# Six V tiles move from ahead of the first score to between the scores

## The chip, the cores and the metric

The kernel runs on one core of a Trainium2 chip. The metric is the device time of one execution in microseconds (us), the median of the runs shown. The core has five engines that work side by side, each with a queue of its own that it works off in order: TensorE (PE) does matmuls, VectorE (DVE) and ScalarE (ACT) work on tiles and read the matmuls' results from PSUM, GpSimd (POOL) works on tiles in SBUF, and SyncE (SP) issues nearly all DMAs of this kernel. Engines and DMAs wait for each other by semaphores, which are counters.

## What is computed

The input is x, 2048 tokens of 512 numbers, all in float32. The result mixes an attention block and a gated feed-forward block (FFN), token by token:

```python
g = sigmoid((x * gate_w).sum(-1, keepdims=True))
q, k, v = x @ wqkv, split into 32 heads of 16
a = softmax(q @ k.T * 16 ** -0.5) @ v, heads joined, @ wo
b = (silu(x @ w1) * (x @ w3)) @ w2        # 512 -> 1792 -> 512
out = g * a + (1 - g) * b
```

## The kernel before

**Precision.** A float32 matmul costs more than one in the reduced type float32r. The kernel therefore splits every operand of a large product into a high part (H) and the rest (L) in float32r, and adds three matmuls, H·H, H·L and L·H (`three`, line 93). Rows go through DRAM where another layout is wanted.

**First phase.** x comes in four blocks of 512 tokens (`load_x`). TensorE transposes a block (`transpose_x`), ScalarE and VectorE write its two parts (xH, xL). `project_qk(c, b, w)` computes q and k for 128 columns (chunk c, 8 heads) and block b, ScalarE rounds the high part, VectorE subtracts, and SP stores the four tiles to DRAM (`store_qk`). In the first phase this is done for chunk 0 only, in four calls, one for each block. `project_v(t)` computes V for 128 tokens and all heads in 12 dense matmuls; there are 16 such tiles, and ScalarE copies each into V. For the last three tiles (`last_v`, three PSUM banks) VectorE makes the copies behind the branch below.

**The guard.** The softmax subtracts no row maximum. Instead `bound()` takes an upper bound for all scores from the largest squared norm of a token (`x_squares`) and the weights' column norms (`squares`), and sets a flag. `guard_rows()` writes the bound as two rows per head to a DRAM tensor M. `load_guard` loads them beside the rows of q, where Kt holds -1, so that the score matmul subtracts the bound. `load_q` and `load_k` fetch the H and L rows of two heads from DRAM into the tiles Qt and Kt. Only if the flag is not set, `row_maxima()` (line 275, its branch on line 278) computes true maxima; this branch stands at the end of the first phase and is not taken with these inputs. Its body contains projections, DMAs and a `load_step(0)`, so the engines' semaphores have to agree behind it whether it was taken or skipped. All engines read the flag and branch for themselves.

**The stream.** What follows is a long order of slots, written out by hand as a string. A score is one unit: 128 keys against 512 queries of two heads (line 745), then one exponential on ScalarE (line 749). There are 1024 units, 32 in a step; a step is two heads against half of the queries. The letters are Q (one unit's scores), P (V times the exponentials of two units, line 733, which accumulates in `acc`), and F (`feed`). An F advances two lanes by one matmul each: lane 0 uses the upper 64 rows of the TensorE array, lane 1 the lower 64. A block of n slots is done by one lane for one half of the contraction and then, at least 6 ticks later (GAP), by the other lane for the other half. `blocks()` yields them in order: q and k for chunks 1 to 3, the FFN's w1 and w3 products (chunk by chunk, 12 slots a block), the FFN's second product (the h phase, 14 slots a block), and the first o products. `load_weights` loads the chunks' weights and POOL splits them; chunk 0 of this list is loaded in the first phase, ahead of the branch. `halves_of` and `load_piece` load h and split it on POOL.

One turn of the order is a period of 8 Q and 4 P. A period of kind "one" has 21 F, and one of kind "two" has 15:

```python
LONG, SHORT = 78, 50
one = "QQFFFFFF" + "QFFF" * 5 + "QPPPP"
two = "QFFF" * 5 + "QPPQQPP"
order = one * LONG + "QQFFF" + two * (SHORT - 1) + "QFFF" * 4 + "QPPQPP"
```

Two PSUM tiles hold scores (S), so a third unit's scores need the first one's exponential to be done. Three banks (f) serve the blocks and the V tiles.

**The order around the change.** Behind `project_qk(0, 3)`, SP's queue holds these items, in this order: the stores of block 3, `load_q` and `load_k` for the first step, the two stores of M, the two weight loads of chunk 0, the two guard loads, the branch. TensorE's queue holds V tiles 9 and 10, the matmuls of `bound`, V tile 11, the one of `guard_rows`, and V tiles 12 to 15.

Of the kernel before, what the change touches and what calls it, by code (L numbers as in the profile page):

```python
# [8 lines left out]
F32 = mybir.dt.float32  # L9
# [8 lines left out]
P = 128  # L18
S = 2048
D = 512  # L20
F = 1792
H = 32
DH = 16
NB = S // 512
NT = S // P
ND = D // P
NF = F // P
NPAIR = H // 2
SCALE = DH ** -0.5
SAFE = 64.0  # L30


@with_exitstack
def gated_mix_kernel(ctx: ExitStack, tc: tile.TileContext, x, wqkv, wo, w1, w3, w2, gate_w, out):
# [18 lines left out]
    nc = tc.nc  # L53
# [66 lines left out]
    def load_w(c):  # L120
        w = slot("fr", F32, (P, ND, P))
        nc.sync.dma_start(w, wqkv[:, c:c + P].rearrange("(k p) n -> p k n", p=P))
        return w
# [37 lines left out]
    def x_squares(b):  # L161
        for t in range(4):
            nc.scalar.activation(slot("sg", F32), xn[b][:, t, :], AF.Square, accum_out=x2[:, 4 * b + t:4 * b + t + 1])

    def x_gate(b):
        for t in range(4):
            nc.vector.scalar_tensor_tensor(slot("hx", F32), xn[b][:, t, :], 1.0, gw, op0=OP.mult, op1=OP.mult,
                                           accum_out=z[:, 4 * b + t:4 * b + t + 1])
# [5 lines left out]
    def project_qk(c, b, w, between=None):  # L174
        ps = psum2()
        for i in range(2):
            if i and between:
                between()
            for n, (h, xs) in enumerate(((0, xH), (0, xL), (1, xH))):
                for k in range(ND):  # L180
                    nc.tensor.matmul(ps[:, i, :], w[i][h][:, k, :], xs[b][:, k, :], start=n == k == 0,
                                     stop=n == 2 and k == ND - 1)
        hi = p1.tile([P, 2, 512], F32R, name="hi", bufs=2)
        lo = p1.tile([P, 2, 512], F32R, name="lo", bufs=2)
        nc.scalar.activation(hi, ps, AF.Copy)
        nc.vector.tensor_sub(lo, ps, hi)
        for i in range(2):
            store_qk(i, c, b, hi[:, i, :], lo[:, i, :])
# [20 lines left out]
    def project_v(t):  # L209
        nc.scalar.activation(*sums_v(t), AF.Copy)  # L210
# [35 lines left out]
            nc.sync.dma_start(M_d[:, a, :].rearrange("h (j t) -> h j t", t=512),  # L246
                              r[a][:].bitcast(F32)[:, None, :].to_broadcast([H, 4, 512]))

    def load_k(j, i):
        for h in range(2):  # L250
            r = 64 * h
            s = slice(DH * (2 * j + h), DH * (2 * j + h) + DH)
            for o, ks in enumerate((0, 0, 1)):
                nc.sync.dma_start(Kt[i][r + DH * o:r + DH * o + DH, :].bitcast(F32), QD[1][ks][s, :])

    def load_q(j, half, i):
        for h in range(2):
# [6 lines left out]
    def load_guard(j, half, i):  # L264
        for h in range(2):
            nc.sync.dma_start(Qt[i][64 * h + 48:64 * h + 50, :].bitcast(F32),
                              M_d[2 * j + h, :, 1024 * half:1024 * half + 1024])
# [81 lines left out]
    x_gate(1)  # L349
    load_x(3)  # L350
    ws = [load_w(P * c) for c in range(1, ND)]
    for t in range(4):
        project_v(t)
    transpose_x(2)
    fill_k()
    project_v(4)
    for c in range(1, ND):
        squares(ws[c - 1], c)
    x_squares(2)
    project_qk(0, 2, wq)  # L360
    x_gate(2)
    ws = [load_w(D + P * c) for c in range(1, ND)]
    for t in range(5, 8):
        project_v(t)
    transpose_x(3)
    project_v(8)
    for c in range(1, ND):
        squares(ws[c - 1], ND + c)
    x_squares(3)
    project_qk(0, 3, wq)  # L370
    load_q(0, 0, 0)
    load_k(0, 0)
    project_v(9)
    project_v(10)
    bound()
    project_v(11)
    guard_rows()
    x_gate(3)
    load_weights(chunks[0])

# [1 line left out]
    nc.vector.tensor_scalar(g, g, 1.0, None, op0=OP.add)  # L382
    nc.vector.reciprocal(g, g)
    nc.vector.tensor_scalar(omg, g, -1.0, 1.0, op0=OP.mult, op1=OP.add)
    load_guard(0, 0, 0)
    for t in range(12, NT - 3):
        project_v(t)

    last_v = [sums_v(t) for t in range(NT - 3, NT)]
    row_maxima()  # L390
    for to, src in last_v:
        nc.vector.tensor_copy(to, src)  # L392
# [12 lines left out]
    def w_product(chunk, which, b):  # L405
        def product(ps, r, n, second):
            w = chunk["w"][which]
            k, i = divmod(n, 3)
            return nc.tensor.matmul(ps, w[i == 2][r, k, :], (xL if i == 1 else xH)[b][r, k, :],  # L409
                                    start=n == 0 and not second, stop=n == 3 * ND - 1 and second)  # L410
        return product

    qk_left = 8 * (ND - 1)

# [226 lines left out]
                    yield  # L641

    def blocks():
        last = len(chunks) - 1
        turns = [(m, b) for m in range(last - 1) for b in range(NB)]
        turns += [(last - i, b) for two in ((0, 1), (2,), (3,)) for i in (1, 0) for b in two]
        for m, b in turns:
            for which in range(2):
                if m < ND - 1:
                    yield w_product(chunks[m], which, b), qk_done(m + 1, which, b), 3 * ND  # L650
                else:
                    yield w_product(chunks[m], which, b), (up_done if which else gate_done)(m - ND + 1, b), 3 * ND
                if (b, which) == (1, 0) and m < last - 1 or (m, b, which) == (last - 1, 0, 1):
                    load_weights(chunks[m + 1])
        for t in range(NT):
            for part in range(3):
                yield h_product(t, part), h_done(t, part), PART
        for t in range(NT // 2 - 2):
            yield o_product(t), o_done(t), 3 * ND

    NBLOCK = 8 * len(chunks) + 3 * NT + NT // 2 - 2
    source = blocks()

    REST, GAP = 9, 6
# [89 lines left out]


    NP = 8
    LONG, SHORT = 78, 50
    one = "QQFFFFFF" + "QFFF" * 5 + "QPPPP"
    two = "QFFF" * 5 + "QPPQQPP"
    order = one * LONG + "QQFFF" + two * (SHORT - 1) + "QFFF" * 4 + "QPPQPP"  # L760
# [4 lines left out]
    for i, c in enumerate(order):  # L765
        clock += 1 if c != "P" else 4
        if c == "Q":
            step = issued // 32 + 1
            if issued % 32 == 6 and step < 2 * NPAIR:
                assert 8 * (ND - 1) - qk_left >= 8 * min(step // 4, ND - 1)  # L770
                load_step(step)
            pend.append(score(*next(units)))
            issued += 1
            while soon and order[i + 1] == "P":
                soon.pop(0)()
            if issued % 128 == (40 if issued // 128 == 5 else 12) and 1 <= issued // 128 < 8:
                stages.append(divide((issued // 128 - 1) % 4, (issued // 128 - 1) // 4))
            if small or later and hurry:
                for _ in range(3 if hurry else 1 + (len(small) > (6 if len(over) < 8 * len(chunks) - 16 else 0))):
                    if small or later and hurry:  # L780
                        (small or later).pop(0)()
            if loads and (hurry or issued % 2 or len(over) > 8 * len(chunks) - 12):
                loads.pop(0)()
            for stage in stages[:1]:
                if next(stage, stages) is stages:
                    stages.pop(0)
        elif c == "F":
            feed()
        else:
            pv(pend[:2])  # L790
            pend = pend[2:]
# [78 lines left out]
```

## Time and profile before

| | |
|---|---|
| median of 3 runs | 1413.47 us (1412.27 to 1413.79) |
| the profiled execution | 1409.74 us |
| its span, first to last instruction | 1408.0 us |
| TensorE busy | 1399.5 us, 99% of the span |
| ScalarE busy | 1033.5 us, 73% |
| VectorE, GpSimd busy | 483.3 us (34%), 318.7 us (23%) |

All rows of the profile come from the one profiled execution. A row of the timeline gives the start in us from the span's start, the time from the first start to the last end, the engine, the line of the kernel, the operation, what it writes and reads, and how many instructions were merged; in brackets stands how long the engine sat idle before it and who ended that. "SPq" and "POOLq" mark instructions of the queue itself, such as the issue of a DMA, which are not counted as busy time. A row of a line's instructions gives shortest, middle and longest duration in ns, and the first and last start in us. A row of the windows gives, for a stretch of time, the busy time of PE, of its weight loads (PEld), of DVE, ACT and POOL, then the share of the full TensorE clock that was granted, the share of the DMA engines and GB/s.

### The profile page before, as it was taken

The numbers are of one execution on the slowest core, as the hardware profiler recorded it, in microseconds if no ns is written. First come the engines' busy times: TensorE is split into PE (matmuls) and PEld (weight loads), VectorE is DVE, ScalarE is ACT, GpSimd is POOL, SyncE is SP. The second block draws the span as 40 slices with busy tenths as digits, with TensorE's granted clock in tenths as the row PEclk, the third lists the DMA queues.
The fourth block names the chain that finished last, engine by engine and source line by source line (L and its number), as shares of the span: only waits on it lengthen the run. The fifth ranks groups of instructions, "written<-read, shape, count | busy, mean of one in ns | idle before, by whom it ended". The sixth has DMA issues, their size and how long they took to land.

```text
span 1408.0 us, 28877 instructions
## 1 busy us (share of the span) xinstructions
PE 1399.5 (99%) x11399; PEld 826.9 (59%) x11399; DVE 483.3 (34%) x1067; ACT 1033.5 (73%) x1153; POOL 318.7 (23%) x356
## 2 busy tenths in 40 slices
PE   9999999999999999999999999999999999999998
PEld 7866556656556556556566566555555555555556
DVE  5421111565555545545464554411110110110113
ACT  4547767777777777777777777788788778877880
POOL 5024443011011101110110115441223332232240
PEclk9999999999999999999999999999999999999999
DMA  7553564243123433233332246443534433354445
GB/s 195 147 129 108 125 148 122 56 126 75 38 66 86 113 55 76 58 74 91 77 76 62 82 82 156 111 106 79 124 88 91 109 105 71 69 129 109 104 120 178
DMA packets 112671, 141.44 MB, mean 100 GB/s; under 512 B 16400, under 2 KB 70672, under 8 KB 109456
## 3 DMA queue, kind: packets, MB, share of 16 engines
q1 hardware_dynamic: 110384, 135.72, 39.8%
q10 hardware_dynamic: 2144, 3.80, 0.8%
q8 instruction: 92, 1.51, 0.5%
q14 instruction: 51, 0.42, 0.1%
HBM read 90.70 MB, written 48.76 MB: 99 GB/s over the span
## 4 chain that ended last, share of the span: by engine, by line
PE 93%; DVE 0%; POOL 0%; DMA 0%; issue 0%; ACT 0%; DVEq 0%; POOLq 0%; ACTq 0%
PE acc L733 33%; PE f L409 27%; PE S L745 20%; PE f L524 11%; PE f L610 1%; PE f L95 0%; PE f L96 0%; PE f L97 0%; PE S L97 0%; PE S L96 0%; PE S L95 0%; DMA kL_d<-gs 0%; DVE V L392 0%; POOL gs L422 0%; ACT p L749 0%
## 5 line engine op out<-in xcount | busy, mean ns | idle before, releaser
L749 ACT ACTIVATE p<-S 128x1024 f32<-128x1024 f32 x1024 | 967.9, 1025 | 300.7 <-PE S L745 300.7
L733 PE MATMUL acc<-p,V 128*17 128x512 f32 x4096 | 474.4, 594 | 0.0
L745 PE MATMUL S<-Qt,Kt 50*128 50x512 f32 x2048 | 408.3, 411 | 1.0 <-DVE V L392 0.7
L745 PEld LDWEIGHTS S<-Qt,Kt 50*128 50x128 f32 x2048 | 183.9, 184 | 183.2 <-ACT p L749 85.0
L733 PEld LDWEIGHTS acc<-p,V 128*17 128x17 f32 x4096 | 102.2, 97 | 273.9 <-issue 273.6
L440 DVE RECIPROCAL sg<-sg 128x64 f32<-128x64 f32 x448 | 209.3, 517 | 49.2 <-issue 47.1
L409 PE MATMUL f<-xH,fh 64*128 64x512 f32 x1024 | 205.0, 390 | 0.5 <-DVE tick L706 0.5
L409 PE MATMUL f<-xL,fh 64*128 64x512 f32 x1024 | 205.1, 391 | 0.0
L409 PE MATMUL f<-xH,fl 64*128 64x512 f32 x1024 | 204.7, 390 | 0.0
L321 POOL CAST fh<-fr 128x512 fp32r<-128x512 f32 x32 | 19.9, 621 | 427.9 <-DMA fr<-in_B_w_dram 335.0
L409 PEld LDWEIGHTS f<-xH,fh 64*128 64x128 f32 x1024 | 99.1, 186 | 22.6 <-DVE tick L706 0.9
L409 PEld LDWEIGHTS f<-xL,fh 64*128 64x128 f32 x1024 | 99.5, 187 | 20.9
L409 PEld LDWEIGHTS f<-xH,fl 64*128 64x128 f32 x1024 | 98.3, 184 | 20.1
L706 DVE MEMSET tick<- 1x1 f32 x190 | 11.2, 59 | 273.5 <-PE f L524 156.1
L524 PE MATMUL f<-xH,fl 64*128 64x512 f32 x224 | 65.8, 390 | 0.0
L524 PE MATMUL f<-xL,fh 64*128 64x512 f32 x224 | 64.6, 390 | 0.0
L524 PE MATMUL f<-xH,fh 64*128 64x512 f32 x224 | 64.0, 391 | 0.0
L432 DVE COPY gs<-f 128x512 f32<-128x512 f32 x56 | 38.7, 691 | 69.6 <-PE f L409 63.3
L524 PE MATMUL f<-xH,raw 64*128 64x512 f32 x192 | 56.6, 390 | 0.0
L438 DVE TENSOR_SCALAR sg<-sg 128x512 f32<-128x512 f32 x56 | 27.7, 495 | 83.2 <-ACT sg L437 81.1
L714 DVE COPY u<-acc 128x512 f32<-128x512 f32 x32 | 22.1, 692 | 95.2 <-PE acc L733 88.9
L543 DVE SCALAR_TENSOR_TENSOR y<-f,omg,y 128x512 f32<-128x512 f32 x32 | 24.0, 751 | 82.9 <-PE f L524 82.9
(217 smaller groups left out, 1335.2 us busy)
## 6 DMA issues: line engine op xcount, KB each, us to landing
Kt<-kH_d SPq DMA_DIRECT2D x128, 128.0 KB
h_d<-sg SPq DMA_DIRECT2D x56, 256.0 KB
sg<-h_d SPq DMA_DIRECT2D x43, 256.0 KB
fr<-in_B_w_dram SPq DMA_DIRECT2D x42, 256.0 KB
Qt<-qH_d SPq DMA_DIRECT2D x128, 64.0 KB
Kt<-kL_d SPq DMA_DIRECT2D x64, 128.0 KB
fr<-in_A_wqkv_dram SPq DMA_DIRECT2D x18, 256.0 KB
Qt<-qL_d SPq DMA_DIRECT2D x64, 64.0 KB
```

The source lines that it names most:

```text
L321: nc.gpsimd.tensor_copy(wh, r)
L409: return nc.tensor.matmul(ps, w[i == 2][r, k, :], (xL if i == 1 else xH)[b][r, k, :], start=n == 0 and not second, stop=n == 3 * ND - 1 an ...
L432: nc.vector.tensor_copy(gs, ps)
L438: small.append(lambda: nc.vector.tensor_scalar(sg, sg, 1.0, None, op0=OP.add))
L440: small.append(lambda q=q: nc.vector.reciprocal(sg[:, q:q + 64], sg[:, q:q + 64]))
L524: ins = nc.tensor.matmul(ps, hs[t][q][i == 2][r, P * o:P * o + P], (w2L if i == 1 else w2H)[q][r, o, :], start=n == 0 and not second, stop ...
L543: nc.vector.scalar_tensor_tensor(y, ps, omg[:, t:t + 1], y, op0=OP.mult, op1=OP.add)
L610: return nc.tensor.matmul(ps, ot[t][i == 2][r, P * k:P * k + P], wo_[k][i == 1][r, :], start=n == 0 and not second, stop=n == 3 * ND - 1 a ...
L714: nc.vector.tensor_copy(u, acc)
L733: nc.tensor.matmul(acc[r:r + DH + 1, :], V[:, k, 2 * j + h, :], p[:, h, :], start=k == 0, stop=k == NT - 1)
L745: nc.tensor.matmul(ps[:, h, :], Kt[i][r:r + 50, P * k:P * k + P], Qt[i][r:r + 50, t:t + 512], start=True, stop=True)
L749: nc.scalar.activation(p, ps, AF.Exp, scale=SCALE)
```

## The change

The first phase computes V tiles 0 to 9 instead of 0 to 15. Tiles 10 to 15 become the first six blocks of the stream, 12 slots each, with their copies on VectorE. The order has 12 more periods of kind "one" and 12 fewer of kind "two", so that there are 72 more F. Conditions that counted blocks up to the end of the FFN's first products use `FIRST`, which includes the six.

The first phase is put in another order. `project_qk(0, 2)` comes ahead of the squares of the query weights, and only tiles 0 to 6 stand ahead of `project_qk(0, 3)`. `bound()` is called between the two halves (q and k) of that last projection. `load_q` and the first three blocks' columns of K are issued ahead of it, and the fourth block's columns behind it, so K takes 12 DMAs instead of 6. The guard loads come right behind M's stores, and the second piece of K and the weight loads of chunk 0 behind those. Tiles 7, 8 and 9 are now the ones whose copies stand behind the branch.

```diff
+EARLY_V = 10
-    def load_k(j, i):
+    def load_k(j, i, b0=0, b1=NB):
+        c = slice(512 * b0, 512 * b1)
...
-                nc.sync.dma_start(Kt[i][r + DH * o:r + DH * o + DH, :].bitcast(F32), QD[1][ks][s, :])
+                nc.sync.dma_start(Kt[i][r + DH * o:r + DH * o + DH, c].bitcast(F32), QD[1][ks][s, c])
...
-    for t in range(4):
+    for t in range(3):
         project_v(t)
     transpose_x(2)
     fill_k()
-    project_v(4)
+    project_v(3)
+    x_squares(2)
+    project_qk(0, 2, wq)
     for c in range(1, ND):
         squares(ws[c - 1], c)
-    x_squares(2)
-    project_qk(0, 2, wq)
+    ws = [load_w(D + P * c) for c in range(1, ND)]
     x_gate(2)
-    ws = [load_w(D + P * c) for c in range(1, ND)]
-    for t in range(5, 8):
-        project_v(t)
+    project_v(4)
+    x_squares(3)
+    project_v(5)
     transpose_x(3)
-    project_v(8)
+    project_v(6)
     for c in range(1, ND):
         squares(ws[c - 1], ND + c)
-    x_squares(3)
-    project_qk(0, 3, wq)
     load_q(0, 0, 0)
-    load_k(0, 0)
-    project_v(9)
-    project_v(10)
-    bound()
-    project_v(11)
+    load_k(0, 0, 0, 3)
+    project_qk(0, 3, wq, bound)
     guard_rows()
+    load_guard(0, 0, 0)
+    load_k(0, 0, 3, NB)
     x_gate(3)
     load_weights(chunks[0])
...
-    load_guard(0, 0, 0)
-    for t in range(12, NT - 3):
-        project_v(t)
-
-    last_v = [sums_v(t) for t in range(NT - 3, NT)]
+
+    last_v = [sums_v(t) for t in range(7, EARLY_V)]
     row_maxima()
...
+    def v_product(t):
+        b, o = divmod(P * t, 512)
+
+        def product(ps, r, n, second):
+            k, i = divmod(n, 3)
+            return nc.tensor.matmul(ps, (xL if i == 2 else xH)[b][r, k, o:o + P], wv[k][i == 1][r, :],
+                                    start=n == 0 and not second, stop=n == 3 * ND - 1 and second)
+        return product
+
+    def v_done(t):
+        return lambda ps: nc.vector.tensor_copy(V[:, t, :, 0:DH], ps.rearrange("p (h d) -> p h d", d=DH))
...
     def blocks():
+        for t in range(EARLY_V, NT):
+            yield v_product(t), v_done(t), 3 * ND
...
-    NBLOCK = 8 * len(chunks) + 3 * NT + NT // 2 - 2
+    FIRST = NT - EARLY_V + 8 * len(chunks)
+    NBLOCK = FIRST + 3 * NT + NT // 2 - 2
...
-    LONG, SHORT = 78, 50
+    LONG, SHORT = 90, 38
```

More of the change, by code (lines that the diff above doesn't have):

```diff
@@ L778, in gated_mix_kernel @@
             if small or later and hurry:
-                for _ in range(3 if hurry else 1 + (len(small) > (6 if len(over) < 8 * len(chunks) - 16 else 0))):
+                for _ in range(3 if hurry else 1 + (len(small) > (6 if len(over) < FIRST - 16 else 0))):
                     if small or later and hurry:
                         (small or later).pop(0)()
-            if loads and (hurry or issued % 2 or len(over) > 8 * len(chunks) - 12):
+            if loads and (hurry or issued % 2 or len(over) > FIRST - 12):
                 loads.pop(0)()
```

## The prediction

> **What bounds the kernel now.** I read the page first (busy time, then the chain that ended last), then the order of time on TensorE to get the price of one period, and last each queue around the first score, because the change moves work from ahead of the first score to behind it.
>
> ```profile
> PE 1399.5 (99%) x11399; PEld 826.9 (59%) x11399; DVE 483.3 (34%) x1067; ACT 1033.5 (73%) x1153; POOL 318.7 (23%) x356
> PE 93%; DVE 0%; POOL 0%; DMA 0%; issue 0%; ACT 0%; DVEq 0%; POOLq 0%; ACTq 0%
> ```
>
> TensorE (PE) is busy 99% and is 93% of the chain that ended last. So each matmul slot counts, wherever it stands, and a piece of work is only cheaper if it costs fewer TensorE microseconds in its new place. The price of a period is read from the bursts of PV matmuls (line 733), one a period in the first kind ("one"), two in the second ("two"); a period of both kinds does 8 scores and 4 P.
>
> ```profile
> 879.43 3.63 PE L733 MATMUL acc<-p,V 128*17 128x512 f32 x32
> 889.92 3.63 PE L733 MATMUL acc<-p,V 128*17 128x512 f32 x32
> ...
> 1005.06 1.91 PE L733 MATMUL acc<-p,V 128*17 128x512 f32 x16
> 1014.48 1.91 PE L733 MATMUL acc<-p,V 128*17 128x512 f32 x16
> ```
>
> "One" with 21 F takes 889.92 - 879.43 = 10.49 us; "two" with 15 F takes 1014.48 - 1005.06 = 9.42 us. Six more F cost 1.07 us.
>
> **The stream: what is added.** The count of F slots goes from 78 x 21 + 3 + 49 x 15 + 12 = 2388 to 90 x 21 + 3 + 37 x 15 + 12 = 2460: 72 more, which is 6 V tiles x 12 slots. Twelve periods turn from "two" into "one", at 12 x 1.07 = **+12.84 us**. The slots left over (12) and the tail behind the periods are the same.
>
> **The front: what is removed.** The copies that follow each V tile of the first phase (line 210) give the dense price of a tile.
>
> ```profile
> 29.35 0.60 ACT L210 ACTIVATE V<-f 128x512 f32<-128x512 f32 x1 [2.20 <-PE f L97]
> 32.15 0.60 ACT L210 ACTIVATE V<-f 128x512 f32<-128x512 f32 x1 [2.20 <-PE f L97]
> ```
>
> 2.80 us a tile, so six tiles are 16.80 us of TensorE ahead of the first score. If the first score could start that much earlier, the change would gain 16.80 - 12.84 = 3.96 us. Whether it can is the question; TensorE's own rows around the first score are these.
>
> ```profile
> 63.45 0.40 PE L95 MATMUL f<-fh,xH 128*128 128x512 f32 x1
> 68.82 0.40 PE L97 MATMUL f<-fh,xL 128*128 128x512 f32 x1
> 69.37 0.48 PE L95 MATMUL f<-fh,xH 128*128 128x512 f32 x1
> 83.61 0.40 PE L97 MATMUL f<-fh,xL 128*128 128x512 f32 x1
> 84.74 0.93 PE L745 MATMUL S<-Qt,Kt 50*128 50x512 f32 x4 [0.73 <-DVE V L392]
> 86.71 0.59 PE L745 MATMUL S<-Qt,Kt 50*128 50x512 f32 x2
> 91.78 3.63 PE L733 MATMUL acc<-p,V 128*17 128x512 f32 x32
> ```
>
> The last dense V tile ends at 84.0 and the first score starts at 84.74, the first PV burst at 91.78. `project_qk(0, 3)` ended at 63.45, and behind it stood 7 V tiles (19.6 us). In the new order only three stand there (8.4 us), and what those seven covered comes into the open. That cover was for SP's queue and the branch of `row_maxima` (line 278).
>
> ```profile
> 66.81 0.45 SPq L172 DMA_DIRECT2D kL_d<-lo  x1
> 74.83 0.84 SPq L246 DMA_DIRECT2D m_d<-sg  x2
> 75.72 2.19 SPq L314 DMA_DIRECT2D fr<-in_A_wqkv_dram  x2
> 79.39 0.61 SPq L266 DMA_DIRECT2D Qt<-m_d  x2
> 84.58 0.32 SPq L261 DMA_DIRECT2D Qt<-qH_d  x1
> ...
> 88.44 0.94 SPq L254 DMA_DIRECT2D Kt<-kH_d  x2
> 91.28 0.59 SPq L266 DMA_DIRECT2D Qt<-m_d  x2
> ```
>
> ```profile
> L278 SPq EVENT_SEMAPHORE  x8: 17/17/17, 84.0 to 84.5; - x8
> L278 SPq COMPARE_BRANCH  x1: 50/50/50, 81.3 to 81.3; - x1
> L278 POOLq EVENT_SEMAPHORE  x1: 17/17/17, 84.4 to 84.4; - x1
> ```
>
> What to see: the branch body holds DMAs that write Qt and Kt, and when it is skipped each engine raises the counts that the body would have raised. For SP these are eight semaphores, one for each of its DMA counters, each after that counter's earlier DMAs have landed. The first score waits for them (the program lists all eight counters ahead of it; the trace names POOL's semaphore of 84.4, one of a group that came together), so it can't start until SP has worked through everything ahead of the branch: the guard rows and the first weights included. From the guard loads' end (80.0) to the eight (84.5) SP needs 4.5 us, of which 2.7 lie between branch and first semaphore. Before, that ended 0.5 us behind TensorE's own work: the two were balanced, so an advance of TensorE alone is worth nothing.
>
> **SP's chain in the new order, step by step.**
>
> (a) End of `project_qk(0, 3)`: two V tiles fewer ahead of it, 63.45 - 5.60 = 57.85; `bound` in its middle costs 0.55 - 0.23 = 0.32 (68.82 to 69.37 against a step of 0.23, 2.80/12); and I add 0.4 for the key squares, which now end just before it (0 to 1). 58.5.
>
> (b) Guard rows. VectorE (DVE) rows:
>
> ```profile
> 64.70 1.22 DVE L186 TENSOR_TENSOR lo<-S,hi 128x1024 fp32r<-128x1024 f32 x1 [3.65 <-ACT hi L185]
> 72.65 0.14 DVE L240 COPY mm<-f 32x1 f32<-32x1 f32 x1 [2.23 <-PE f L239]
> 73.62 0.47 DVE L244 TENSOR_SCALAR sg<-sg,mm 32x512 fp32r<-32x512 f32 x1
> ```
>
> `lo` ends 2.47 behind the projection, the guard rows take 74.09 - 72.65 = 1.44 behind `lo`: 58.5 + 0.2 + 3.91 = 62.6. SP has just issued the block's stores then (before: 67.26 - 63.45 = 3.81 behind the projection, 62.3). M goes out at 62.6 to 63.5.
>
> (c) M's landing. Before: second issue near 75.28, wait over at 79.39, 4.1 us with K loads ahead in the DMA queues; now 1 MB of stores stands ahead. The lower bound is a lone load of the same 256 KB:
>
> ```profile
> 886.80 0.37 SPq L490 DMA_DIRECT2D fr<-in_B_w_dram  x1
> ...
> 889.63 0.61 POOL L491 CAST xH<-fr 128x512 fp32r<-128x512 f32 x1 [4.25 <-DMA fr<-in_B_w_dram]
> ```
>
> 2.8 us. With the stores ahead I take 4.1: the guard loads go at 67.2 (65.9 at the least).
>
> (d) Behind them now stand, still ahead of the branch, the second piece of K (6 issues, 88.44 to 91.28 = 2.84 us before) and the two weight loads of chunk 0. Before, these weights filled M's landing time; now they come after it. 67.2 + 0.61 + 2.84 = 70.65; the weights at 0.55 each (1.1, nearer to the row below, whose queue is not backed up, than to the 2.19 above):
>
> ```profile
> 52.06 1.65 SPq L122 DMA_DIRECT2D fr<-in_A_wqkv_dram  x3
> ```
>
> 71.75. (e) Then the 4.5 us of the branch: 76.3, and the score 0.2 behind: **76.5 instead of 84.74, -8.2 us**, although TensorE's dense work ends at 58.5 + 8.4 = 66.9 (with `guard_rows`' matmul 67.2). TensorE stands still for some 9 us.
>
> (f) POOL. The weights' split is also ahead of the branch on POOL, and the tile of the first exponential stands where the phase-1 tiles stood, which the skipped body would have written from POOL: that exponential waits for POOL's semaphore of line 278.
>
> ```profile
> 80.44 0.61 POOL L321 CAST raw<-fr 128x512 fp32r<-128x512 f32 x1 [43.46 <-DMA fr<-in_A_wqkv_dram]
> 83.06 1.28 POOL L322 TENSOR_TENSOR gw<-fr,raw 128x512 fp32r<-128x512 f32 x1
> 85.60 7.44 ACT L749 ACTIVATE p<-S 128x1024 f32<-128x1024 f32 x8 [7.96 <-PE S L745]
> ```
>
> First weight issue 70.65, landing 2.8 (alone) to 4.7 (before: 75.72 to 80.44), then 84.34 - 80.44 = 3.9 of POOL: 77.4 to 79.3. The exponential would start at 76.5 + 0.86 = 77.4 anyway. So 0 to 1.9 us of delay for the third score; I take 0.3, near the lone landing, as little else is under way.
>
> (g) The clock after the stop. TensorE's first and its last rows, and its clock behind the last (the seventh column of the windows):
>
> ```profile
> 1.55 3.52 PE L334 MATMUL acc<-ident 128*128 128x128 f32 x18 [1.55 <-DVE acc L330]
> 6.87 1.04 PE L334 MATMUL acc<-ident 128*128 128x128 f32 x8
> 1403.42 0.39 PE L97 MATMUL S<-wo,p 128*128 128x512 f32 x1
> 1404.00:1408.00 4.00, 0.00 (x0) 0.00 (x0) 0.60 (x1) 0.00 (x0) 0.00 (x0) 0.91 0.54 207
> ```
>
> Mean 0.91 over 4 us of idleness is half speed for the last 0.7, so the clock fell some 3.5 us after the last matmul; and from a cold start 18 transposes took 3.52 us where the later rate (a step of 0.11) makes 2.1. A stop of 9 us should cost that **1.4 us** again; bounds 0 (it doesn't fall) and 1.4.
> [...]
>
> **Costs at nothing.** Six evacuations move from ScalarE to VectorE, 0.7 us each in 34 us; VectorE is 34% busy. PV of a step's last k tiles needs tile 15 before the burst behind F 84; two lanes of 12 slots a half finish it near F 78, and tiles 10 and 11 by F 36 of 42. The FFN blocks come 72 slots later, as do their ends: the 756 slots behind them are as before, only that their first 9 periods now run at 21 F. Loads there have the time of two h tiles, 40 us at the new rate. Weights of chunk 0 are used 72 slots later. Squares moved behind the projection free its evacuation.
>
> **Sum.** +12.84 - 8.2 + 0.3 + 1.4 = +6.3 us. The profiled execution took 1409.74 (span 1408.0), 3.7 under the median of 1413.47: 1416.0 for it, **1419.8** for the median.
>
> **Rivals.**
> *The front is TensorE's (faster side).* If SP isn't late, the first score follows the dense work: -16.80 + 0.3 + 12.84 = -3.7, 1409.8. For it: before, only 0.73 us lay between. Against: six K issues, two weight loads and the branch, 8.4 us by rows, stand serially behind M's landing. It decides from a first score at 71.9 on (84.74 - 12.84): 4.6 earlier than my chain. Chance 0.10.
> *SP's chain is half as late.* M lands in 2.8, the weights' issue or the branch's 4.5 us are partly overlapped, no cold clock: first score near 72.5 to 74, +0.6 to +2.1, 1414 to 1415.6. Chance 0.13.
> *The clock stays up*, chain as reckoned: +4.9, 1418.4. For it: no stop inside the kernel shows in the trace; against it the drop at the end. Chance 0.15.
> *POOL is late* by its upper bound, 1.9, and the squares by 1: +6.3 + 1.6 + 0.6 = +8.5, 1422. Chance 0.14.
> *The h phase starves* in its nine faster periods (TensorE waits for h pieces, 1 us a period): +15, 1429. The trace has no such wait. Chance 0.05.
> *My forecast*, 1419.8: chance 0.43. Its own range runs from all low bounds (-1.3 at M, -1.4 clock, -0.7 squares and POOL: 1416.4) to the high ones (1424).
>
> A difference within 0.2% (2.8 us) can't be told from no change. Faster 0.10; same 0.15 (the half-late chain and a little); slower 0.75. The range 1412 to 1424 leaves out the TensorE-bound front and the starving h phase.
>
> **What the profile would show.** First PV burst near 85.5 (91.78 before); TensorE idle 8 to 10 us behind the third dense V tile, ended by SP's line 278; clock under 1 in the window behind; SP's branch near 73; period lengths unchanged, 90 of 10.49. The prediction is wrong if the first score comes by 72, if SP's eight come early while the score waits for something else, or if the periods change their length.

## The result, and the profile after

The changed kernel takes 1437.92 us (median of 4 runs, 1436.01 to 1439.41) where the kernel before takes 1412.87 (1410.79 to 1413.79): a ratio of 1.0181, 95% interval 1.0168 to 1.0193. It is slower, as forecast, but by 25 us and not by 6.3, and lies outside the range of 1412 to 1424. The profiled execution took 1436.01 us with a span of 1434.2, that is 26.2 more span than before. TensorE is busy 98% of it (99% before), but the chain that ended last now holds other engines:

```profile
PE 1403.3 (98%) x11471; PEld 835.6 (58%) x11471; DVE 485.7 (34%) x1079; ACT 1029.5 (72%) x1147; POOL 317.5 (22%) x356
...
PE 92%; DMA 1%; POOL 1%; SPq 0%; issue 0%; ACT 0%; DVE 0%; POOLq 0%; DVEq 0%; ACTq 0%
```

The waits of TensorE in the stream (from 90 to 1400 us; columns: who waited for whom, us in total, how often, the longest) say at once that this is no longer a kernel whose TensorE never stands still. Before:

```profile
PE f L409 <- DVE tick L706: 0.5, 1, 0.5
PE S L745 <- ACT p L749: 0.3, 1, 0.3
```

After:

```profile
PE f L533 <- POOL fh L500: 5.6, 1, 5.6
PE f L406 <- DVE tick L718: 4.8, 1, 4.8
```

Two waits are new, each a single one. Their price is read from the bursts of PV matmuls (line 745 now), one a period, in TensorE's order of time (start, duration):

```profile
90.83 1.48 PE L745 MATMUL acc<-p,V 128*17 128x512 f32 x12
...
185.41 3.63 PE L745 MATMUL acc<-p,V 128*17 128x512 f32 x32
201.83 2.56 PE L745 MATMUL acc<-p,V 128*17 128x512 f32 x16
212.97 2.34 PE L745 MATMUL acc<-p,V 128*17 128x512 f32 x20
...
947.61 3.63 PE L745 MATMUL acc<-p,V 128*17 128x512 f32 x32
965.76 4.60 PE L745 MATMUL acc<-p,V 128*17 128x512 f32 x32
977.23 3.20 PE L745 MATMUL acc<-p,V 128*17 128x512 f32 x28
```

I count periods from 0 at the first burst. Nearly all take the 10.49 or 9.42 us of before; periods 9 and 10 take 16.42 + 11.14, and 81 and 82 take 18.15 + 11.47. Behind each stop the granted clock is at half, from 199.8 to 203.2 and from 961.0 to 967.8, so the period behind it is long as well. TensorE worked 3.4 us at half rate behind its wait of 4.8 us, and 5.4 us behind that of 5.6; with half of this work lost, 4.8 + 1.7 = 6.5 and 5.6 + 2.7 = 8.3, close to the prices of the two stops in the table. The 26.2 us divide as follows.

| place | forecast | measured | from |
|---|---|---|---|
| first PV burst | -6.5 | -0.95 | 90.83 - 91.78 |
| 12 periods of the other kind | +12.84 | +12.84 | 12 x 1.07 |
| stop in periods 9 and 10 | 0 | +6.6 | 27.56 - 2 x 10.49 |
| stop in periods 81 and 82 | 0 | +8.6 | 29.62 - 2 x 10.49 |
| a small stop of before in period 6, gone | 0 | -0.8 | 10.49 - 11.26 |

The sum is 26.3. The term that I had costed best, the stream, came out as reckoned; the gain of the front is nearly nothing, and two stops stand where I wrote "at nothing".

**The front.** SP's queue, and the branch of `row_maxima` (line 280 now; its rows are instruction, count, duration, first and last start):

```profile
63.93 1.01 SPq L247 DMA_DIRECT2D m_d<-sg  x2
68.76 0.96 SPq L268 DMA_DIRECT2D Qt<-m_d  x2
...
73.45 0.97 SPq L316 DMA_DIRECT2D fr<-in_A_wqkv_dram  x2
...
81.17 1.42 PE L757 MATMUL S<-Qt,Kt 50*128 50x512 f32 x4 [12.21 <-SPq L280]
```

```profile
L280 SPq EVENT_SEMAPHORE  x8: 17/17/17, 78.4 to 80.9; - x8
L280 SPq COMPARE_BRANCH  x1: 50/50/50, 75.3 to 75.3; - x1
```

The chain is the forecast one, with the wait for SP's eight semaphores at its end (12.21 us of TensorE idle), but the score comes at 81.17 and not at 76.5. The first of the eight stands 3.0 us behind the branch (2.7 before); the other seven follow 2.0 us later, where before all eight came within 0.5. No DMA explains this second gap: the last one issued ahead of the branch had landed at 77.5, and the profile puts both gaps down to SP itself. And the clock (the number before the last two columns):

```profile
73.00:76.00 3.00, 0.00 (x0) 0.00 (x0) 0.13 (x1) 0.00 (x0) 0.00 (x0) 0.58 0.53 147
...
82.00:85.00 3.00, 3.00 (x17) 3.00 (x16) 0.00 (x0) 1.94 (x2) 0.00 (x0) 0.50 0.26 63
85.00:88.00 3.00, 3.00 (x20) 2.95 (x18) 0.06 (x1) 1.71 (x2) 0.00 (x0) 0.64 1.01 197
```

It is at half some 4.5 us behind the last dense matmul and stays there till 87.1 (0.64 x 3 us), 6 us behind the first score. From the first score to the first PV burst it takes 9.66 us; before, 91.78 - 84.74 = 7.04.

**The first stop.** POOL and VectorE (in brackets: idle time of the engine ahead of this row, and what ended it):

```profile
190.74 0.61 POOL L323 CAST fh<-fr 128x512 fp32r<-128x512 f32 x1 [12.30 <-DMA fr<-in_A_wqkv_dram]
...
194.59 0.62 POOL L430 CAST sg<-gs 128x512 fp32r<-128x512 f32 x1
195.29 1.26 POOL L431 TENSOR_TENSOR gs<-gs,sg 128x512 f32<-128x512 f32 x1
```

```profile
199.08 0.69 DVE L429 COPY gs<-f 128x512 f32<-128x512 f32 x1 [7.20 <-DMA kL_d<-gs]
199.71 0.06 DVE L718 MEMSET tick<- 1x1 f32 x1
...
199.82 0.80 PE L406 MATMUL f<-xH,fh 64*128 64x512 f32 x2 [4.77 <-DVE tick L718]
```

POOL waits 12.3 us for the weights of the next chunk. Behind that split stands, in POOL's order, the split of a finished q or k block (lines 430 and 431); VectorE's third copy (line 429) needs one of the two gs buffers, which come free when that split is stored; the memset that hands a bank to the other half of TensorE's array (line 718) stands behind the copy; TensorE waits for the memset. What made the weights late is SP's order:

```profile
178.47 0.32 SPq L173 DMA_DIRECT2D qL_d<-gs  x1
178.88 0.38 SPq L263 DMA_DIRECT2D Qt<-qH_d  x1
...
184.41 0.57 SPq L268 DMA_DIRECT2D Qt<-m_d  x2
185.03 1.15 SPq L316 DMA_DIRECT2D fr<-in_A_wqkv_dram  x2
```

All 14 loads of the next step stand ahead of them.

**The second stop.** POOL waits for the last FFN block, because its next job writes the tile (xH) that the block still reads; then TensorE, which is in the h phase already, waits for pieces of h that stand behind that job:

```profile
952.44 0.61 POOL L500 CAST xH<-fr 128x512 fp32r<-128x512 f32 x1 [12.44 <-PE f L406]
...
961.74 0.61 POOL L500 CAST fh<-fr 128x512 fp32r<-128x512 f32 x1
962.40 0.79 PE L533 MATMUL f<-xH,fh 64*128 64x512 f32 x1 [5.63 <-POOL fh L500]
```

From 952.44 to 961.74 POOL works through four other splits. Before, the same place was passed at 15 F a period; now its first nine periods run at 21.

### The profile page after: what moved, and what is told of

Same layout as the page of the kernel before. It is cut to its first block, busy times and chain, and to the rows that moved or that the text cites. A ratio compares the mean times of both kernels' runs of the same rounds, so it can differ in the third digit from the quotient of the medians.

```text
span 1434.2 us, 29035 instructions
## 1 busy us (share of the span) xinstructions
PE 1403.3 (98%) x11471; PEld 835.6 (58%) x11471; DVE 485.7 (34%) x1079; ACT 1029.5 (72%) x1147; POOL 317.5 (22%) x356
## 4 chain that ended last, share of the span: by engine, by line
PE 92%; DMA 1%; POOL 1%; SPq 0%; issue 0%; ACT 0%; DVE 0%; POOLq 0%; DVEq 0%; ACTq 0%
PE acc L745 32%; PE f L406 26%; PE S L757 19%; PE f L533 11%; PE f L415 1%; PE f L619 1%; DMA fr<-in_A_wqkv_dram 0%; PE f L96 0%; PE f L97 0%; PE f L98 0%; PE S L98 0%; PE S L97 0%; PE S L96 0%; DMA sg<-h_d 0%; SPq L256 0%
## 5 line engine op out<-in xcount | busy, mean ns | idle before, releaser
L757 PE MATMUL S<-Qt,Kt 50*128 50x512 f32 x2048 | 410.8, 412 | 12.5 <-SPq L280 12.2
L757 PEld LDWEIGHTS S<-Qt,Kt 50*128 50x128 f32 x2048 | 186.9, 185 | 185.1 <-issue 76.5
```

The lines of the kernel that those rows point to most:

```text
L757: nc.tensor.matmul(ps[:, h, :], Kt[i][r:r + 50, P * k:P * k + P], Qt[i][r:r + 50, t:t + 512], start=True, stop=True)
```

## The experiments

Each edit is against the changed kernel unless it says otherwise. A total given without a ratio is one execution, and those of the kernel before spread over 4.6 us; so there the argument goes by the rows of the trace. First the three delays, one at a time.

**The pace at the start of the h phase.** The nine periods by which LONG exceeds the start of the h phase go to a later place.

```
-    order = one * LONG + "QQFFF" + two * (SHORT - 1) + "QFFF" * 4 + "QPPQPP"
+    twos = lambda n: "QQFFF" + two * (n - 1) + "QFFF" * 4 + "QPPQPP"
+    order = one * 81 + twos(SHORT // 2) + one * (LONG - 81) + twos(SHORT - SHORT // 2)
```

> The changed kernel with the same 90 and 38 periods in another order: 81 of the first kind (1701 F plus the 3 of the joint, where the first products of the FFN end at F 1704), then 19 of the second, 9 of the first, 19 of the second. Theory A (the h phase starts at 21 F to 8 Q, and loads that are taken one per Q fall behind the F that use them; POOL then splits pieces that are used later first): periods 81 and 82 (18.15 and 11.47 us in the changed kernel) go back to their usual length, -8.6 us. Rival B (the stop comes from POOL's wait for the last FFN block, whatever the pace): the stop stays, 0 us.

Measured: 1432.71 us, beside 1413.26 for the kernel before on the same chip, although first burst (91.55) and first stop (16.24 + 12.0) were a little worse than in the changed kernel. TensorE's waits in the stream:

```profile
PE f L406 <- DVE tick L718: 4.8, 2, 4.6
PE f L533 <- POOL fl L501: 1.7, 1, 1.7
```

The wait for h falls from 5.6 to 1.7, and of the 8.6 us only 1.9 are left, in period 82 (11.33). POOL waited no less for the last FFN block than before the edit (13.4 us, 12.4 before). So that wait alone is not the stop; it becomes one when TensorE runs through its h blocks at 21 F a period while POOL catches up.

**SP's chain ahead of the first score.** The second piece of K and the first weights go behind the branch.

```
-    load_k(0, 0, 3, NB)
     x_gate(3)
-    load_weights(chunks[0])
...
     ph1.close()
+    load_k(0, 0, 3, NB)
+    load_weights(chunks[0])
```

> The changed kernel with the second piece of K and the first weight loads behind the branch, so that on SP nothing but the guard loads stands between M and the branch. Theory A (the first score waits for all that stands ahead of the branch in SP's queue): the branch comes right behind the guard loads, some 4.5 us earlier, and the first score at 74 to 77 instead of 81.17; the first PV burst 4 to 7 us earlier. Rival B (the score waits for the split weights on POOL or for the second piece of K): it moves by less than 2 us.

```profile
L280 SPq EVENT_SEMAPHORE  x8: 17/17/17, 73.7 to 74.3; - x8
L280 SPq COMPARE_BRANCH  x1: 50/50/50, 70.9 to 70.9; - x1
...
74.57 0.99 PE L757 MATMUL S<-Qt,Kt 50*128 50x512 f32 x2 [5.47 <-SPq L280]
```

Measured: 1429.96 us, first score 6.6 us and first burst (84.10) 6.7 us earlier. The eight semaphores came in 0.6 us here, without the second gap. This is the chain that I had forecast: SP's branch comes 4.4 us earlier (70.9 for 75.3), which is the price of what stood in (d) of the prediction, and nearly all of the rest is the second gap. In the five traces whose front is the changed kernel's own, the first burst lies anywhere from 90.07 to 94.07, so the gain is larger than this scatter. The stretch from score to burst is still 9.53.

**The clock.** Two versions put transposes of the identity where TensorE stands idle. The first puts 90 ahead of the branch in the changed kernel.

```
+    idle(90)
     row_maxima()
```

> The changed kernel with 90 transposes of the identity (0.11 us each) between the last dense V tile and the branch, so that TensorE doesn't stand still. If the half clock costs what I read (first score to first PV burst 9.66 us against 7.04 before), that distance falls to 7.0 to 7.5, -2.2 to -2.6 us, with the first score still near 81. If the distance has another cause (the first exponential, the V blocks), it stays at 9.7.

Measured: 1440.16 us. The transposes ended at 79.35, the first score came at 82.22, and in the 2.87 us between the clock fell all the same, to half from 81.6 to 88.4; the stretch was 9.74. With the clock down in spite of the cover, this run couldn't tell the theories apart. The second takes the front version just shown and puts 34 transposes behind the branch.

```
     row_maxima()
+    idle(34)
```

> The front version (second piece of K and first weights behind the branch) with 34 transposes of the identity on TensorE behind the branch's place in its queue, so that TensorE isn't idle from the branch to the first score (about 4 us at 0.11 us each). Theory A (the clock's fall behind the stop is what stretches the stretch from the first score to the first PV burst, 9.53 against 7.04 us before): the first score stays near 74.6, the stretch shortens to 7.0 to 8.0 us, no or little half clock after 75, time 1427.5 to 1428.5 (front version 1429.96). Rival B (the stretch is long for another reason, the exponentials or the slots fed in it): 9.3 us or more, time within 0.5 us of the front version, whether the clock falls or not.

```profile
68.81 0.40 PE L98 MATMUL f<-fh,xL 128*128 128x512 f32 x1
71.10 2.92 PE L336 MATMUL acc<-ident 128*128 128x128 f32 x25 [1.89 <-PEq L280]
74.61 1.20 PE L336 MATMUL acc<-ident 128*128 128x128 f32 x9 [0.59 <-issue]
75.74 0.50 PE L758 MATMUL S<-Qt,Kt 50*128 50x512 f32 x2
...
82.71 1.48 PE L746 MATMUL acc<-p,V 128*17 128x512 f32 x12
```

```profile
70.00:76.00 6.00, 4.31 (x36) 3.94 (x38) 1.89 (x3) 0.00 (x0) 0.00 (x0) 1.00 0.07 16
76.00:80.00 4.00, 4.00 (x35) 3.23 (x34) 0.07 (x2) 3.56 (x4) 0.00 (x0) 1.00 0.21 42
```

The front version's row for the same stretch:

```profile
76.00:80.00 4.00, 4.00 (x21) 4.00 (x20) 0.00 (x0) 2.65 (x3) 0.00 (x0) 0.50 0.21 47
```

The clock stays whole and the stretch is 6.97 us, where the front version had 9.53: the fallen clock costs 2.6 us at this place, all of the difference to before. The time as a whole, 1429.86, missed its forecast and didn't fall with it: the first score came 1.2 later, and periods 9 and 10 took 17.47 + 12.65 here, 2.6 more than in the front version. There TensorE waited 5.8 us in place of 4.8, and the clock was at half for 10.2 us in place of 3.4. The stretch is what this run tells, not the total.

**The first stop.** Three versions try its cause. The loads of a step go out eight units later:

```
-            if issued % 32 == 6 and step < 2 * NPAIR:
+            if issued % 32 == 14 and step < 2 * NPAIR:
```

> The changed kernel with the loads of the next step issued 8 units later (at unit 14 instead of 6 of a step), so that the weight loads of the last q and k chunk stand ahead of a step's 14 loads in SP's queue instead of behind. Theory A (weights late behind the step's loads, POOL held by them, the block's split and with it VectorE's copy and its tick late): periods 9 and 10 (16.41 and 11.14 us) go back to about 10.5, -6.6 us. Rival B (the stop comes from the 72 slots' delay of the q and k blocks as such): it stays or moves to another period with a like size.

Measured: 1437.87 us. Periods 9 and 10 are normal, but period 6 now takes 15.78: there the 14 loads stand right ahead of a store of k, from 150.66 to 156.75, and the same chain of gs buffer, copy and memset follows. The stop moved. In the new place POOL waits only 4.1 us for weights, but VectorE's copy waits 9.2 us for the store of k behind the loads. The total didn't fall because the stop at periods 81 and 82 grew too, to 21.58 + 11.04, 3.0 more than in the changed kernel. A stop needs a meeting of the 6 us of loads with the q/k work; which of the two hands does the harm at periods 9 and 10, SP's long burst or POOL's wait, was open. Next, the loads go out in six portions, one a unit (the drip functions load q, k or the guard for one head):

```
...
-                load_step(step)
+                half, j = divmod(step, NPAIR)
+                drip[:] = [lambda h=h, j=j, half=half, i=step % 2, f=f: f(j, half, i, h)
+                           for f in (drip_q, drip_k, drip_guard) for h in range(2)]
+            if drip:
+                drip.pop(0)()
```

> The changed kernel; the 14 loads of each next step go out in six portions, one a score unit from the seventh unit on, and not in one go. Theory A (the stop at periods 9 and 10 comes from SP: 6 us of issuing in one go hold up the weights or the stores of q and k behind them, then POOL's split, then VectorE): both periods take their usual 10.49 us (16.41 and 11.14 before, 0.5 us each way), no other period gains over 1 us, the stop at 81 and 82 stays; time 1437.9 - 6.6 = 1431 to 1432.5. Rival B (the collision isn't SP's: POOL's own backlog of weights and q/k halves at that place): a stop of 4 us or more stays in periods 5 to 18, time 1436 or more.

Measured: 1440.87 us, periods 9 and 10 at 16.51 and 11.08. I missed. The burst was no burst of the program's making: SP stood behind the store of q until 182.2, which waits for POOL, and by then nearly all portions had queued up. (The first burst also came 3.2 later than in the changed kernel, which this edit doesn't explain.) What was left is POOL's wait: the weights are asked for some 5 us before they can land, and the split already stands in POOL's order. So only their load was moved, two blocks ahead of the split:

```
+    def fetch_weights(chunk):
+        chunk["raw"] = [slot("fr", F32, (P, ND, P)) for _ in range(2)]
+        for r, w in zip(chunk["raw"], chunk["src"]):
+            nc.sync.dma_start(r, w.rearrange("(k p) n -> p k n", p=P))
...
+                if (b, which) == (0, 0) and m < last:
+                    fetch_weights(chunks[m + 1])
                 if (b, which) == (1, 0) and m < last - 1 or (m, b, which) == (last - 1, 0, 1):
                     load_weights(chunks[m + 1])
```

> The changed kernel; the loads of the next chunk's weights go out when the first block of a chunk is taken up, and only GpSimd's split of them stays at its old place, two blocks later (some 12 us). Theory C (formed after the run with portions, where SP's queue stood behind the q store until 182 and the weights still came behind all 14 loads: the stop at periods 9 and 10 is GpSimd's wait of 12.3 us, in its order, for weights that were asked for 4.6 us before they landed; the q/k splits stand behind it, VectorE's third copy waits for one of the two buffers, TensorE for the memset behind that copy): GpSimd's wait there is put down to a copy and not to the weights' landing, periods 9 and 10 take 10.4 to 11 us, time 1430.5 to 1432. Rival D (GpSimd simply has too much to do at that place: four weight halves ahead of four q/k halves, 3.8 us, whenever they land): at least half of the stop stays, 1434.5 or more.

```profile
174.55 2.12 SPq L315 DMA_DIRECT2D fr<-in_A_wqkv_dram  x2
179.56 0.61 POOL L328 CAST fh<-fr 128x512 fp32r<-128x512 f32 x1 [1.81 <-DMA fr<-in_A_wqkv_dram]
...
184.68 3.63 PE L752 MATMUL acc<-p,V 128*17 128x512 f32 x32
195.16 3.63 PE L752 MATMUL acc<-p,V 128*17 128x512 f32 x32
```

Measured: 1430.16 us, period 9 at 10.48 and the next as long. The weights now go out ahead of the step's loads, POOL's wait falls from 12.3 to 1.81 us and the stop is gone. POOL does the same four operations in the same place of its order, so it isn't too much work that stopped TensorE but the wait. The traces of this version and of the changed kernel differ by 5.9 us of span: -6.6 for periods 9 and 10, -0.8 for the first burst, and +1.5 for a new small stop in period 17 (11.97).

**The order of the first phase alone.** All sixteen V tiles dense and 78 and 50 periods, as before; the new order and K in two pieces stay.

```
-    EARLY_V = 10
-    LONG, SHORT = 90, 38
+    EARLY_V = 16
+    LONG, SHORT = 78, 50
```

> The new order of the first phase and K in two pieces stay; all sixteen V tiles are dense again (7 to 12 ahead of the guard rows' end, 13 to 15 last) and the periods are 78 and 50 as before. Theory A (the six V tiles in the stream carry the loss: their slots, the pace and the place they push the other blocks to; the new order costs TensorE nothing once it has cover): the first score follows the dense work, 68.56 + 6 x 2.80 = 85.4, so 85 to 86 us; no stop of over 2 us in any period; time within 3 us of before (1410 to 1416). Rival B (the new order itself is late, whatever covers it): SP's chain of 81.17 slides with the projections and the first score comes after 88; time 1416 or more.

Measured: 1413.91 us, beside 1412.53 for the kernel before. First score 86.84, 0.8 behind the last dense matmul, first burst 93.87, no stop at either place, and the stop of before in period 6 longer (12.91, so 2.4 where I had forecast none over 2). With the dense tiles to cover it the new order costs little, 2.1 us at the first burst in this trace and nothing clear of the spread in the total; both stops come with the six V tiles in the stream.

**Put together.** The first attempt joined the pace, the front, the portions, and guard rows ahead of the rounding and subtracting behind the last projection.

> All remedies together: 81 first periods and 19 of the second kind, then 9 and 19 (h phase at the slow pace), second piece of K and first weights behind the branch, guard rows ahead of the last projection's halves, next step's loads in portions; the six V tiles stay in the stream. Theory A (the changed kernel's loss is these three delays and the front): no stop of over 2 us; first score 70 to 73, first PV burst 78 to 82; against before 12.84 for the periods less 10 to 14 for the first burst less 0.8: 1411 to 1417, that is the same as before within 0.3%. Rival B (each remedy moves its stop elsewhere): a stop of over 4 us in some period and 1420 or more.

Measured: 1425.32 us, ratio 1.0089 (1.0076 to 1.0103). The forecast of 1411 to 1417 missed. First score at 73.44 and first burst at 83.24, 0.4 and 1.2 us beyond their forecasts, no stop at the h phase beyond 2.0, but periods 9 and 10 at 15.5 and 11.71: the portions were the wrong remedy, as above. With the right one, and the transposes, but no change to the guard rows:

> The changed kernel with its ten dense V tiles and all that removed a delay alone: second piece of K and first weights behind the branch, 34 transposes up to the first score, weights' loads two blocks ahead of their split, h phase begun at the slow pace (81, 19, 9, 19). Theory A (the delays are separate and add up): first PV burst near 82.7, no stop in periods 6 to 11 and none at the h phase's start beyond 1 us; from the version with the weights ahead, 1430.2, less 90.07 - 82.71 = 7.4 and less 7.9 at the h phase: 1414.9, between 1413 and 1417, at most 0.3% over before. Rival B (a removed delay only uncovers another): 1419 or more.

Measured: 1416.19 us, ratio 1.0026 (1.0017 to 1.0035). The first burst is at 82.82, and TensorE's waits in the stream are these:

```profile
PE f L539 <- POOL fl L507: 1.6, 1, 1.6
PE f L412 <- DVE tick L726: 1.2, 1, 1.2
```

The delays are separate and add up: the time is in the range of theory A, though the 1.8 us at period 82 are more than the 1 us that it allowed. The two large terms of the sum are now 12.84 for the periods and -9.0 for the first burst. What is left beside them are 1.8 at period 82 and 1.7 at period 17 (12.16), whose cause I did not follow. So even with its delays removed the change doesn't pay: 0.26% slower than before.

**Twelve dense V tiles.** Two more tiles where TensorE stands idle, so 86 and 42 periods.

```
-    EARLY_V = 10
-    LONG, SHORT = 90, 38
+    EARLY_V = 12
+    LONG, SHORT = 86, 42
```

(with 80, 21, 6 and 21 periods in turn, the front, the early guard rows, and the weights' loads ahead of their split)

> Twelve of the sixteen V tiles dense, four in the stream (86 and 42 periods: 80, 21, 6 and 21), with the weights' loads ahead of their split, second piece of K and first weights behind the branch, guard rows ahead of the last projection's halves. Two dense tiles more end at 68.3 + 5.6 = 73.9, about where SP's eight semaphores came (73.1): TensorE has work up to there. Theory A (loss and gain are those of this document): first score 74 to 75, full clock, first PV burst 81 to 82.5, which is 9.3 to 10.8 earlier than before; 8 periods of the first kind more, 8 x 1.07 = 8.56 later; no stop of over 1.5 us: faster than before by 0.5 to 3 us, 1409.5 to 1412 where before is 1412.5. Rival B (the stops move to other places, or the first score slips again with what TensorE does): 1414 or more.

Measured: 1425.2 us, ratio 1.009 (1.0076 to 1.0103). I missed at both ends. The first burst came at 87.26, with the clock at half from 76.8 to 83.6. The first score came at 77.62, 2.94 us behind the dense work, though SP's semaphores were there at 73.4; the trace names a load of K, but TensorE's own branch had ended only at 74.3, and which of the two it was stays open. And the h phase stopped for longer than ever, at the slow pace:

```profile
PE f L541 <- POOL fh L508: 8.3, 1, 8.3
```

There a step's 14 loads (924.5 to 931.9) stood ahead of the w2 and h loads on SP, and POOL waited 16.9 us. This suggests that the slow pace is a remedy only where no burst of loads meets the start of the phase; no run tells the two apart.

**The remedy on the kernel before.** Only the weights' loads ahead of their split, edited into the kernel before.

> The kernel before, with the loads of the next chunk's weights put two blocks ahead of their split as in the run that took the stop out of the changed kernel. Theory C (GpSimd's wait for weights just asked for is a stop wherever SP's order puts them behind a step's loads; before had one small one, period 6 with 11.26 instead of 10.49): period 6 takes 10.5, all else is as before: 0.8 us faster, 1411 to 1412.3 where before is 1412.6. Rival (the weights, now earlier, push the loads of a step or a store back): a period of over 11 us elsewhere, 1413 or more.

```profile
154.96 3.63 PE L740 MATMUL acc<-p,V 128*17 128x512 f32 x32
165.46 3.63 PE L740 MATMUL acc<-p,V 128*17 128x512 f32 x32
```

Measured: 1409.8 us (1409.13 to 1410.71, 11 runs) beside 1412.3 (1410.23 to 1414.82, 21 runs): ratio 0.998 (0.9971 to 0.9989), faster than both kernels. Period 6 takes 10.50. I had forecast 0.8 and 1411 to 1412.3, so the gain of 2.5 us is larger than its theory. The two traces don't show it: their spans differ by 0.3 us (1407.7 and 1408.0), and the profiled execution of before, 1409.74, was shorter than all 21. The gain goes with the spread, which shrinks from 4.6 to 1.6 us, and with the clock: of the 21, the five above 1413.5 us had a granted clock of 0.998 or 0.999, the seven under 1412 had 1.000 but for one, and the eleven here have 0.999 or 1.000. A stop in period 6 that is longer in other executions, and then brings the clock down, would do this; no trace of one was taken, so it is not shown.

## Why the prediction was wrong

**Right.** TensorE is the bound, and twelve periods cost 12.84: all but the four periods of the two stops kept their length, on the mean to 0.02 us. TensorE stood idle behind the third dense V tile, ended by SP's line 280, for 12.2 us where I had 8 to 10. The mechanism of the front and its order of links held, and the rival of a TensorE-bound front is out (the first score didn't come by 72). That the kernel is slower was forecast, but from a sum that held a quarter of the loss; more than half of it came from places that I had put at nothing, so the direction proves little.

**Wrong: "Costs at nothing".** This is the step that failed, with 15 of the 20 us by which the sum was short. I wrote of the FFN blocks, which come 72 slots later, that the slots behind them are as before and that loads have the time of two h tiles; of the q and k blocks, where the first stop stands, I wrote nothing, and of the weights I named only those of chunk 0. I checked time and not order. What moved is the place of every chunk's blocks against the steps, whose loads are tied to the score units. At one meeting of the two, weights went out behind 14 loads, and POOL's wait for them (12.3 us) reached TensorE over three engines: +6.6. And I named the starving h phase as a rival, with 1 us in each of nine periods, +15, chance 0.05. It is real, but it is one stop of 8.6 at the start, where POOL catches up on what it couldn't do while the last FFN block ran. The sentence "the trace has no such wait" was true and no argument: before ran this place at 15 F a period. The trace of before even showed the other mechanism in small, with period 6 at 11.26; I had read period lengths from undisturbed bursts only.

**Wrong: the size of the front.** First burst -0.95 in place of -6.5. By the steps: (a) the projection ended near 60.1 where I had 58.5. The key squares had to wait for their weights, and the matmul of `bound` in the middle of the projection waited for them:

```profile
55.40 0.63 ACT L222 ACTIVATE raw<-fr 128x512 f32<-128x512 f32 x1 [0.55 <-DMA fr<-in_A_wqkv_dram]
56.89 0.27 PE L230 MATMUL f<-rs,V 128*1 128x64 f32 x2 [1.60 <-DVE am L227]
```

(b) and (c) kept that delay: M went out from 63.93 (62.6 forecast), the guard loads at 68.76 (67.2). From M's second issue, near 64.4, to the guard loads 4.3 us passed, where I took 4.1. (d) K and weights took 73.45 + 0.97 - 69.72 = 4.7, where I had 3.94: the fourth and fifth K issue took 1.76. (e) From there to the score 6.75 us and not 4.7: the second gap of 2.0 in SP's eight. (f) POOL was no part of it. (g) The clock cost 2.6 and not 1.4. I had taken the price from the kernel's first 18 transposes, 3.52 us in place of 2.1; but the windows of before read 1.00 there (0 to 8 us), so those rows showed no half clock. Here the clock stayed at half for 6 us of work. Together these are 1.6 at the guard loads, 1.1 in (d), 2.0 in (e) and 1.2 in (g), less the 0.3 of (f): the 5.6 us by which the front was late. What the second gap is stays open: no run here shows what SP did in it.

The range missed for two reasons. The front alone, 5.6 us later, would have made 1425.4, just above its 1424: (a), (d), (e) and (g) took longer than their bounds or had none. And a stop that I held for nothing had no bound at all; that is where most of the distance comes from.

## What to carry to other kernels

When work is moved between two streams that run at different rates, such as blocks against steps, list anew what meets what on every in-order queue: a burst of loads ahead of a load that another engine's next job waits for cost 0.8 us at one meeting here (period 6 of before) and 6.6 us at another (periods 9 and 10). A load should be asked for well ahead of the instruction that waits for it, because that wait also holds what stands behind it in the queue, as POOL's 12.3 us held the split of the q and k blocks; here this took a stop of 6.6 us out of the changed kernel and 0.2% out of the kernel before. A cover of zero price is to be checked at its own pace: ask which rate the stretch had when it showed no wait.

## What the runs showed of the hardware

Three stops of TensorE cost more than their length. Behind 12.21 us of idleness the clock stayed at half for 6 us of work, a loss of 2.6 us; behind the waits of 4.77 and 5.63 us it was at half for another 3.4 and 5.4 us of work, by the estimate above a loss of 1.7 and 2.7. In the covered front version an idle 1.89 us was followed by 34 transposes, and the clock read 1.00 from 70 to 84 us; in the version with 90 transposes ahead of the branch an idle 2.87 us came behind 10 us of transposes, and the clock was at half from 81.6 to 88.4.

How long the clock stays at half differs from stop to stop. In the trace of the changed kernel it is at half from 73.49 to 87.14, from 199.78 to 203.20 and from 960.95 to 967.78, that is for 13.65, 3.42 and 6.83 us. Stops of 4.8, 4.6 and 5.8 us at the same place (changed kernel, pace version, covered front) came with 3.4, 6.8 and 10.2 us at half. So the length of a stop did not tell its price here; what does, no run shows.

And a branch that was passed over came with a second gap in its queue: between SP's first and second semaphore behind it lay 2.0 us in the changed kernel, with the eight from 78.4 to 80.9, and no such gap in the front version, with the same eight instructions from 73.7 to 74.3.

Of float32 beside float32r the trace of before shows this: the PV matmuls (float32, 512 columns) stand there as 4096 records for 2048 calls, 474.4 us busy, and the scores (float32r, 512 columns) as 2048 records for 2048 calls, 408.3 us. No run has one product in both types.
